# Zeros for empty rows in another buffer, and a later due time for transposes of gathered rows

## The chip, the cores and the metric

The kernel runs on one core of a Trainium2 chip. The metric is the device time of one execution in microseconds (us); the time before is the median of three runs. Matrix products run on TensorE (PE in the profile; PEld is its weight load), elementwise work on VectorE (DVE), ScalarE (ACT) and GpSimd (POOL). SyncE (SP) issues most of the DMAs, ScalarE's and GpSimd's queues issue some.

## What is computed

The reference has three stages, for 4 batches of 576 rows (2304 rows in all, 512 wide):

```
attn = attention(q, k, v, phi)              # 8 heads of 64, 32 memory slots
u    = x + real(fft over rows and columns)  # x: the heads side by side
un   = layernorm(u)
x2   = u + max(un @ w_ch1, 0) @ w_ch2       # 512 -> 2048 -> 512
e    = expert of each row: argmax of x2 @ w_gate, or the expert
       of the row before, by a gate of its own
out  = p[e] * (max(x2 @ w1[e], 0) @ w2[e])  # 8 experts, 512 -> 1024 -> 512
```

Each row goes through one expert, so the third stage sorts the rows by expert while the program runs.

## The kernel before, in words

**Products.** Precision is kept by splitting both factors into a high part of a shorter type and the rest. Every product is three matmuls (`products`, lines 1022 to 1026): high by high, high by low, low by high. A first-layer step of an expert is 12 matmuls of 256 columns, a second-layer step is 3 matmuls of 512 columns.

**Attention and Fourier stage.** For each batch, `front` (line 384 on) makes the keys and values of the memory, transposes the keys into kT (copied by ScalarE, line 446) and multiplies them with q (line 463, q loaded at line 373); `soft` (line 473 on) takes the scores through a softmax, beginning with a VectorE maximum (line 511); `back` and `mix` do the rest and write u to device memory. Meanwhile `chunks` (line 632 on) loads the weights of the second stage, which come in 64 bits: `fetch` (lines 201 to 209) takes one of the two buffers of the pool `stg` and issues a load of 512 KB on SP (line 205); ScalarE and VectorE turn it into 32 bits (lines 666 to 670, VectorE's two steps into a buffer `sw`), GpSimd multiplies the sign back, and the result is split into high and low part. Two such tasks run side by side, so the first two loads are due early.

**The zeros.** `start` (line 691 on) fills 520 columns of a buffer with zeros and stores them, on ScalarE's queue, into the last 256 rows of ys and one row behind them (lines 700 and 701). ys (N + 1 rows of 520) later takes the second stage's rows; a place of an expert's block that no row fills reads row N, so that row must hold zeros. Before, the buffer with the zeros is a buffer of the pool `stg`: the second load of weights takes the same buffer and waits on SP's queue until the stores have landed. In SP's program the order at the start is: two ph loads, two kv loads, first and second weight load, q of batch 0, third weight load, fourth weight load, and then ph, kv and q of batch 1.

**XL.** The rows of a block, turned so that the width lies on the partitions, stand in XH (high part) and XL (low part), two of each, 128 x 4 x 256. XH[0] and XL[0] are first written by `prep` for the first 256 rows, when attention and mixing are nearly done (`first_rows`, line 724).

**The experts' slots.** After the second stage the rows of each expert are cut into blocks of up to 256, one block a slot. Slots 0 and 1 are woven into the end of the second stage; from slot 2 on there is one piece of program for each slot (lines 1285 on) with two arms, full (256 rows) and narrow (up to 128). The numbers decided on the chip here give 12 slots, 0 to 11; of the ten from slot 2 on, seven are full and three (5, 6 and 11) narrow. A full slot is eight first-layer steps (`firsts`), relu and split by ScalarE and VectorE (`hiddens`), and two halves of eight second-layer steps each (`half_out`), each half ended by a VectorE product (line 1144) and a GpSimd scatter into the output (line 1147). A narrow slot has four first-layer steps with rows and weights exchanged, transposes of the result, and one half.

**What a slot does for the next.** `tokens(j + 1)` runs in slot j. GpSimd issues two indirect DMAs that gather 128 rows each from ys into a buffer of `stg` (line 1253). Each half is then turned by four TensorE transposes into the one PSUM bank pt (`turned4`, lines 288 to 297), copied by ScalarE into XH (line 1261) and subtracted by VectorE into XL (line 1263), and VectorE takes the rows' factor (line 1268). The bank is free for the second half when the subtraction of the first is done. `cuts` splits raw weights, by a ScalarE copy (line 1208) and a subtraction on VectorE or GpSimd (line 1210), and then issues the raw load for the next slot on SP (line 1200). A raw piece so has most of a slot to land.

**What sets the order.** Each engine executes its instructions in the order in which the program issues them, and this order comes from a planner that runs when the program is built (`weave`, lines 230 to 265). Tasks are generators that yield an engine, a cost in us and the planned ends of what the step depends on; the planner keeps a clock for each engine and takes next the step with the smallest planned start plus the task's bias. In the slots the costs are multiplied by SLOT_PACE (TensorE 0.928) and the biases are those of SLOTS (tokens 0.18, first 0.43, out 0.91; in the narrow arm the tokens task has 0.01). The transposes of a half are given the planned end of their gather's issue plus 3.5 as an earliest start. The program waits on the chip for what it really depends on, but in the order of the plan: a transpose that comes up on TensorE before its gather has landed holds every product behind it.

Of the kernel before, what the change touches and what calls it, by code (L numbers as in the profile page):

```python
# [9 lines left out]
F32 = mybir.dt.float32  # L10
# [157 lines left out]
def f32(ap):  # L168
    return ap.bitcast(F32)
# [3 lines left out]
def attention_fourier_experts_kernel(ctx, tc, qT, phi, kv, w1, w2, wg, wgc, wm, cs, cd, c1, c2, midx, out):  # L173
# [24 lines left out]
    stg = ctx.enter_context(tc.tile_pool(name="stg", bufs=2))  # L198
# [16 lines left out]
    def ended(*names):  # L215
        return [end.get(n, 0.0) for n in names]
# [5 lines left out]
    def span(eng, length, deps):  # L222


        start = max([clock.get(eng, 0.0)] + [d + (0.9 if eng == "D" else LAG) for d in deps])
        if eng == "T" and duty.get(start // TICK - 1, 0.0) < 0.375 * TICK:
            length *= 2
        return start, start + length

    def weave(tasks, done=lambda: False):  # L230
# [7 lines left out]
        while state and not done():  # L238
            best = None
            for s in state:  # L240
                while isinstance(s[2], float) or (callable(s[2]) and s[2]()):
                    if isinstance(s[2], float):
                        s[0] = s[2]
                    s[2] = next(s[1], None)
                if s[2] is None or callable(s[2]):
                    continue
                engs, n, deps, *share = s[2]
                n = {e: pace[e] * x for e, x in (n if isinstance(n, dict) else {engs: n}).items()}
                stop, start, eng = min((*span(e, n[e], deps)[::-1], e) for e in engs)
                if best is None or start + s[0] < best[0]:  # L250
                    best = start + s[0], s, eng, start, stop, n[eng] * (share[0] if share else 1.0)
            assert best is not None or all(s[2] is None for s in state)
            if best is not None:
                _, s, eng, start, stop, n = best
                clock[eng] = stop
                if eng == "T":
                    for k in range(int(start // TICK), int(stop // TICK) + 1):
                        part = min(stop, TICK * k + TICK) - max(start, TICK * k)
                        duty[k] = duty.get(k, 0.0) + part * n / (stop - start)
                mark["eng"] = eng  # L260
                try:
                    s[2] = s[1].send(stop + (2.0 if eng == "D" else 0.0))
                except StopIteration:
                    s[2] = None
            state[:] = [x for x in state if x[2] is not None]
# [22 lines left out]
    def turned4(src, e, bank=None, name="pt"):  # L288

        if bank is None:  # L290
            yield lambda: not mark["pt"]
            mark["pt"] = True
        e = yield "T", 0.43, [e] + (ended("pt") if bank is None else []), 0.5
        pt = (bank or ptp).tile([128, 4, 128], F32, name=name)
        for k in range(4):
            T.transpose(pt[:, k], src(k), id_)  # L296
        return pt, e

    def free_pt(e):
        mark["pt"] = False  # L300
        end["pt"] = e
# [35 lines left out]
    XL = [xx.tile([128, 4, 256], FR, name="xl0")]  # L337
# [351 lines left out]
    uu, w2h, w2l = {}, [], []  # L689

    def start():
        zr = stg.tile([128, 1040], F32, name="stg")[:, 0:520]
        yield "G", 0.5, []
        G.memset(zr, 0.0)
        G.memset(qs[:, 0:1], 0.0)
        G.memset(qs[:, 256:257], 0.0)
        yield lambda: ("kv", 0, 1) in end
        yield "D", 1.5, []
        for r in (N - 256, N - 128):
            nc.scalar.dma_start(out=ys[r:r + 128], in_=zr)  # L700
        nc.scalar.dma_start(out=ys[N:N + 1], in_=zr[0:1])
        mark["zr"] = True
# [540 lines left out]
    def tokens(j):  # L1243

        if j >= NS:
            return
        k = (NG + j) % 2
        yield lambda: ("idx", min(j, 2)) in end and (j == 0 or ("x", NG + j - 1) in end)
        x = stg.tile([128, 1040], F32, name="stg").rearrange("p (t c) -> p t c", t=2)
        e = []  # L1250
        for h in range(2):
            e.append((yield "G", 1.04, ended(("idx", min(j, 2)), ("ys", NG - 2 if j < 2 else NG - 1))))
            G.indirect_dma_start(out=x[:, h], out_offset=None, in_=ys, in_offset=IO(ap=idx[:, h, j:j + 1], axis=0),  # L1253
                                 bounds_check=N, oob_is_err=False)
        before = "first", (16 * NG - 17 if j == 0 else FFN - 1 if j == 1 else FFN + 8 * j - 9)
        yield lambda: before in end
        for h in range(2):
            pt, r = yield from turned4(lambda kk: x[:, h, 128 * kk:128 * kk + 128], e[h] + 3.5)
            hs = slice(128 * h, 128 * h + 128)
            r = yield "S", 0.5, [r] + ended(before)  # L1260
            S.copy(XH[k][:, :, hs], pt)
            r = yield "V", 0.62, [r]
            V.tensor_tensor(out=XL[k][:, :, hs], in0=pt, in1=f32(XH[k][:, :, hs]), op=ALU.subtract)
            free_pt(r)
            yield lambda: j < 2 or ("yr", 2 * (NG + j) - 3) in end
            yield "V", 0.07, []
            j8 = sm_.tile([128, 8], F32, name="j8s")
            V.scalar_tensor_tensor(out=j8, in0=x[:, h, 512:520], scalar=1.0, in1=ohs[:, j], op0=ALU.mult,
                                   op1=ALU.mult, accum_out=PV[k][:, h:h + 1])
        end["x", NG + j] = r  # L1270

    def halves(j):
# [5 lines left out]
           "w2": [chunks(extra[i::LANES], (wgt[:, 3 * i:3 * i + 2], wgt[:, 3 * i + 2])) for i in range(LANES)],  # L1278
           "gate": [gates(), gate_weights()], "sum": [sums_out()], "raw": [raws0(), raws(1), raws(2)],
           "tokens": [tokens(0), tokens(1), tokens(2)], "out": [halves(0), halves(1)],  # L1280
           "cut": [cuts(*[(j, c) for j in range(2) for c in range(8)], *[(2, c) for c in range(4)])]})

    bias.update(SLOTS)
    pace.update(SLOT_PACE)
    with ExitStack() as es:
        for j in range(2, NS):
            if j >= FIRST:
                if j == FIRST:
                    n_slots = value(tab[0:1, 2 * NS:2 * NS + 1], NS, mybir.ALL_ENGINES)
                es.enter_context(tc.If(n_slots > j))  # L1290
            half = value(tab[0:1, NS + j:NS + j + 1], 1, mybir.ALL_ENGINES)
            if j + 2 < NS:
                number(j + 2)
            ns = range(FFN + 8 * j, FFN + 8 * j + 8)
            before = dict(clock), dict(end)
            for arm in range(2):
                with (cmp.Else() if arm else tc.If(half > 0)) as cmp:  # L1297
                    own = [{"first": [firsts(ns)], "hidden": [hiddens(ns)], "out": [halves(j)]},
                           {"narrow": [narrow(j)], "turn": [turn(j)], "out": [half_out(j, 0)]}][arm]
                    weave({**own, ("tokens", "rows")[arm]: [tokens(j + 1)],  # L1300
                           ("cut", "late")[arm]: [cuts(*[(j, c) for c in range(4, 8)]), cuts(*[(j + 1, c) for c in range(4)])]})
                after = before if arm == 0 else full
                full = dict(clock), dict(end)
                for mine, theirs in zip((clock, end), after):
                    mine.clear()
                    mine.update(theirs)
                for n in ns:
                    del hid[n]
# [25 lines left out]
```

## Time and profile before

| what | us |
|---|---|
| median of three runs | 875.41 (872.26 to 875.53) |
| the profiled execution's own time | 870.53 |
| its span in the profile | 868.4 |
| TensorE busy | 797.9 (92%) |
| VectorE busy | 581.6 (67%) |
| ScalarE busy | 311.9 (36%) |
| GpSimd busy | 231.3 (27%) |

The mean granted clock of TensorE is 0.973 of full speed (1 is 2.4 GHz, 0.5 is 1.2 GHz). Attention and Fourier stage end at about 150 us, the second stage at about 605 us, and the slots from slot 2 on run from about 630 us to the end.

In the rows below, a window's line has its bounds, its length, the busy time of PE, PEld, DVE, ACT and POOL with the number of instructions in brackets, the granted clock of TensorE, the mean busy share of the 16 DMA engines and what they moved in GB/s. A line of a timeline has start, duration, engine, line of the program, operation, output <- inputs, shape, count and, in square brackets, how long the engine had stood idle and what ended it. A line of waits has the waiting engine and line, what it waited for, and the total, the number and the longest.

### The profile page before, as it was taken

What the parts mean: (1) busy time and instruction counts of PE and PEld (TensorE: products, weight loads), DVE (VectorE), ACT (ScalarE), POOL (GpSimd) and SP (SyncE); (2) the same over time, 40 slices, a digit from 0 to 9 for tenths busy, and PEclk for the clock granted to TensorE, in tenths of its full rate; (3) what the DMA queues carried; (4) which work ended last, traced back from release to release, by engine and by line L of the source; (5) the groups of instructions that cost most, each with busy time, mean ns of one, the idle gap of its engine ahead of it and who ended that gap; (6) DMA issues with size and microseconds to landing.
All of it is one profiled execution on the core that took longest, in us unless ns stands there. A gap on an engine that the chain in (4) does not pass through costs nothing. (4 is left out here: it accounts for less than half of the span.)

```text
span 868.4 us, 14567 instructions
## 1 busy us (share of the span) xinstructions
PE 797.9 (92%) x5376; PEld 690.4 (80%) x5376; DVE 581.6 (67%) x1391; ACT 311.9 (36%) x587; POOL 231.3 (27%) x194
## 2 busy tenths in 40 slices
PE   2399998899999999999999999999989997999993
PEld 1166666698989898988998989889889886888882
DVE  3677787788567867777575766667665466855563
ACT  2264454566211111111111111154445346654452
POOL 2335664588300000000000000053423311333320
PEclk8599999999999999999999999999999999999997
DMA  7976535564220000000000000392776667866655
GB/s 290 334 279 200 191 88 173 158 186 122 65 93 26 25 26 25 26 26 25 26 25 26 25 25 1 112 330 100 235 238 225 213 197 276 269 213 214 210 199 193
DMA packets 36106, 123.93 MB, mean 143 GB/s; under 512 B 5236, under 2 KB 5492, under 8 KB 34218
## 3 DMA queue, kind: packets, MB, share of 16 engines
q1 hardware_dynamic: 30216, 103.74, 35.5%
q0 software_dynamic: 4528, 14.00, 5.0%
q10 hardware_dynamic: 1266, 4.98, 1.7%
q8 instruction: 52, 0.85, 0.4%
q14 instruction: 44, 0.36, 0.1%
HBM read 107.93 MB, written 15.56 MB: 142 GB/s over the span
## 5 line engine op out<-in xcount | busy, mean ns | idle before, releaser
L1026 PE MATMUL pl<-xh,w1l 128*128 128x256 f32 x864 | 242.4, 281 | 0.0
L1024 PE MATMUL pl<-xh,w1h 128*128 128x256 f32 x576 | 162.9, 283 | 2.1 <-DVE xl L327 2.1
L1063 ACT ACTIVATE hh<-pl 128x256 fp32r<-128x256 f32 x144 | 55.4, 384 | 302.5 <-PE pl L1026 251.1
L1026 PEld LDWEIGHTS pl<-xh,w1l 128*128 128x128 f32 x864 | 163.6, 189 | 0.0
L1025 PE MATMUL pl<-xl,w1h 128*128 128x256 f32 x576 | 161.0, 280 | 0.5 <-DVE xl L327 0.5
L1208 ACT CAST w2h<-w1h 128x1024 fp32r<-128x1024 f32 x100 | 103.3, 1049 | 42.0 <-issue 32.9
L1210 DVE TENSOR_TENSOR w1l<-w1h,w2h 128x1024 fp32r<-128x1024 f32 x86 | 103.6, 1222 | 19.4 <-ACT w2h L1208 16.4
L1065 DVE SCALAR_TENSOR_TENSOR hl<-pl,hh 128x256 fp32r<-128x256 f32 x144 | 60.9, 423 | 79.2 <-ACT hh L1063 77.8
L1024 PEld LDWEIGHTS pl<-xh,w1h 128*128 128x128 f32 x576 | 108.3, 188 | 5.5 <-DVE xl L327 2.3
L1025 PEld LDWEIGHTS pl<-xl,w1h 128*128 128x128 f32 x576 | 108.5, 188 | 3.7 <-DVE xl L327 0.8
L1024 PE MATMUL y<-w2h,hh 128*128 128x512 f32 x272 | 108.9, 400 | 1.9 <-ACT hh L1063 1.9
L1026 PE MATMUL y<-w2h,hl 128*128 128x512 f32 x272 | 106.9, 393 | 0.2 <-DVE hl L1065 0.2
L1025 PE MATMUL y<-w2l,hh 128*128 128x512 f32 x272 | 106.7, 392 | 0.0
L778 DVE SCALAR_TENSOR_TENSOR jk<-stg,wgt 128x512 bf16<-128x512 f32 x144 | 99.0, 687 | 2.7
L317 POOL TENSOR_TENSOR rv<-rv,C 128x1 f32<-128x1 f32 x18 | 13.1, 730 | 274.1 <-DVE rv L315 268.9
L1024 PE MATMUL pl<-xh,w2h 128*128 128x256 f32 x288 | 83.4, 290 | 0.5 <-DVE w2l L1065 0.5
L1025 PE MATMUL pl<-xl,w2h 128*128 128x256 f32 x288 | 81.6, 283 | 0.0
L1147 POOL DMA_INDIRECT out_dram<-u,idx x21 | 27.3, 1302 | 154.6 <-DVE u L1144 105.6
L1024 PE MATMUL y<-w2h,w2l 128*128 128x512 f32 x168 | 67.2, 400 | 0.0
L1026 PE MATMUL y<-w2h,w2l 128*128 128x512 f32 x168 | 66.2, 394 | 0.0
L1025 PE MATMUL y<-w1l,w2l 128*128 128x512 f32 x168 | 66.1, 393 | 0.0
L1026 PEld LDWEIGHTS y<-w2h,hl 128*128 128x128 f32 x272 | 51.1, 188 | 12.6 <-DVE hl L1065 1.3
(240 smaller groups left out, 1435.4 us busy)
## 6 DMA issues: line engine op xcount, KB each, us to landing
w1h<-in_wm_dram SPq DMA_DIRECT2D x108, 512.0 KB
stg<-in_w_dram SPq DMA_DIRECT2D x21, 512.0 KB
kvt<-in_kv_dram SPq DMA_DIRECT2D x8, 1290.0 KB
wgt<-in_w_dram SPq DMA_DIRECT2D x11, 512.0 KB
ys<-stg SPq DMA_DIRECT2D x9, 520.0 KB
qt<-in_qT_dram SPq DMA_DIRECT2D x4, 1156.0 KB
ph<-in_phi_dram SPq DMA_DIRECT2D x8, 320.0 KB
u<-ut SPq DMA_DIRECT2D x12, 192.0 KB
```

The lines of the kernel that those rows point to most:

```text
L317: G.tensor_tensor(out=rv, in0=rv, in1=c_("half"), op=ALU.pow)
L778: V.scalar_tensor_tensor(out=jk, in0=yt[:, t, 0:512], scalar=1.0, in1=wgt[:, e], op0=ALU.mult, op1=ALU.mult, accum_out=L[:, t, e:e + 1])
L1024: T.matmul(ps, a[0], b[0], start=first, stop=False)
L1025: T.matmul(ps, a[0], b[1], start=False, stop=False)
L1026: T.matmul(ps, a[1], b[0], start=False, stop=last)
L1063: S.activation(out=hh, in_=ps, func=AF.Relu)
L1065: V.scalar_tensor_tensor(out=hl, in0=ps, scalar=0.0, in1=f32(hh), op0=ALU.max, op1=ALU.subtract)
L1147: G.indirect_dma_start(out=out, out_offset=IO(ap=idx[:, h, j:j + 1], axis=0), in_=o, in_offset=None, bounds_check=N - 1, oob_is_err=False)
L1208: S.copy(WH[c], RAW[c])
L1210: E[mark["eng"]].tensor_tensor(out=WL[c], in0=RAW[c], in1=f32(WH[c]), op=ALU.subtract)
```

## The change

The zeros are written into XL[0], seen as 128 x 1024 of 32 bits, and stored to ys from there; the pool `stg` loses this use, so its two buffers go to the first two weight loads. In `tokens`, the earliest start of the transposes becomes the planned end of the gather's issue plus 6.0 where j is above 2, which is what slots 2 and later run; for j up to 2 it stays 3.5. Line numbers behind the first edit grow by one.

```
@@ -689,7 +689,8 @@
     def start():
-        zr = stg.tile([128, 1040], F32, name="stg")[:, 0:520]
+
+        zr = f32(XL[0]).rearrange("p k c -> p (k c)")[:, 0:520]
         yield "G", 0.5, []
         G.memset(zr, 0.0)
...
@@ -1255,7 +1256,7 @@
         for h in range(2):
-            pt, r = yield from turned4(lambda kk: x[:, h, 128 * kk:128 * kk + 128], e[h] + 3.5)
+            pt, r = yield from turned4(lambda kk: x[:, h, 128 * kk:128 * kk + 128], e[h] + (6.0 if j > 2 else 3.5))
             hs = slice(128 * h, 128 * h + 128)
```

## Rows read from the trace of the kernel before

**Rows 1.** Windows of 10 us: bounds, length, busy (count) by engine, clock, DMA share, GB/s
```profile
30.00:40.00 10.00, 1.53 (x5) 0.83 (x5) 9.55 (x20) 3.70 (x6) 4.38 (x6) 0.50 0.91 349
...
60.00:70.00 10.00, 10.00 (x50) 7.62 (x49) 8.40 (x22) 3.66 (x8) 6.06 (x7) 1.00 0.46 184
```

**Rows 2.** Waits of TensorE from 630 us on: total us, times, longest us
```profile
PE pt L296 <- DMA stg<-ys,idx: 12.0, 12, 2.9
...
PE pl L1026 <- issue: 3.5, 1, 3.5
```

**Rows 3.** Timeline of SP's queue, 2 to 30 us: start, duration, operation
```profile
2.62 13.07 SPq L205 DMA_DIRECT2D stg<-in_w_dram  x2
...
15.74 0.43 SPq L373 DMA_DIRECT2D qt<-in_qT_dram  x1
```

**Rows 4.** Waits of SP's queue, whole execution
```profile
SPq L205 <- DMA ys<-stg: 12.2, 2, 11.5
```

**Rows 5.** Windows of 2 us at the start, columns as rows 1
```profile
8.00:10.00 2.00, 0.54 (x12) 0.51 (x16) 1.37 (x2) 1.33 (x2) 0.00 (x0) 1.00 1.01 428
...
12.00:14.00 2.00, 1.57 (x40) 1.30 (x40) 0.33 (x2) 0.09 (x1) 0.00 (x0) 1.00 0.77 298
...
14.00:16.00 2.00, 0.74 (x4) 0.40 (x4) 1.86 (x4) 1.25 (x2) 1.13 (x2) 1.00 0.02 9
```

**Rows 6.** Timeline of all engines, 0 to 45 us
```profile
13.91 0.66 ACT L666 ACTIVATE stg<-stg 128x512 f32<-128x512 f32 x1 [3.76 <-DMA stg<-in_w_dram]
...
19.31 0.43 DVE L669 TENSOR_SCALAR sw<-stg 128x512 uint32<-128x512 uint32 x1 [3.17 <-DMA stg<-in_w_dram]
...
20.65 0.35 ACT L446 COPY kT<-pfr 128x256 f32<-128x256 f32 x1
...
22.23 1.22 PE L463 MATMUL pfr<-qt,kT 64*32 64x289 f32 x16 [6.89 <-DMA qt<-in_qT_dram]
...
26.56 0.69 DVE L511 TENSOR_REDUCE mx<-sc 97x16 f32<-97x512 f32 x1 [3.83 <-PE sc L505]
```

**Rows 7.** Timeline of TensorE, three windows: transposes in slots 2, 3, 4
```profile
640.07 0.63 PE L296 MATMUL pt<-C,stg 128*128 128x128 f32 x4 [2.85 <-DMA stg<-ys,idx]
...
665.27 0.63 PE L296 MATMUL pt<-C,stg 128*128 128x128 f32 x4 [0.17 <-DMA stg<-ys,idx]
...
690.65 0.63 PE L296 MATMUL pt<-C,stg 128*128 128x128 f32 x4 [1.77 <-DMA stg<-ys,idx]
```

**Rows 8.** Timeline of VectorE from 600 us on
```profile
630.19 0.75 DVE L1144 TENSOR_SCALAR u<-y,pv 128x512 f32<-128x512 f32 x1 [1.42 <-PE y L1026]
...
658.06 0.75 DVE L1144 TENSOR_SCALAR u<-y,pv 128x512 f32<-128x512 f32 x1 [4.81 <-PE y L1026]
...
681.79 0.75 DVE L1144 TENSOR_SCALAR u<-y,pv 128x512 f32<-128x512 f32 x1 [4.80 <-PE y L1026]
...
707.12 0.75 DVE L1144 TENSOR_SCALAR u<-y,pv 128x512 f32<-128x512 f32 x1 [4.82 <-PE y L1026]
...
695.57 0.68 DVE L1263 TENSOR_TENSOR xl<-pt,xh 128x512 fp32r<-128x512 f32 x1
...
720.33 0.68 DVE L1263 TENSOR_TENSOR xl<-pt,xh 128x512 fp32r<-128x512 f32 x1
...
722.71 0.75 DVE L1144 TENSOR_SCALAR u<-y,pv 128x512 f32<-128x512 f32 x1 [0.42 <-PE y L1026]
```

**Rows 9.** Window of 2 us behind the longest wait, columns as rows 1
```profile
642.00:644.00 2.00, 2.00 (x12) 2.00 (x11) 0.55 (x4) 0.85 (x2) 0.00 (x0) 0.50 0.80 270
```

**Rows 10.** Window of slot 8 ahead of its first transposes, columns as rows 1
```profile
765.40:772.60 7.20, 7.20 (x61) 7.10 (x60) 5.11 (x8) 4.27 (x7) 4.67 (x3) 1.00 0.54 152
```

**Rows 11.** The gathers (line 1253), whole execution, issue to landing
```profile
DMA to landing us min/median/max: 3.6/5.6/7.9
```

**Rows 12.** Waits of TensorE in slot 5, then in slot 11
```profile
PE pt L296 <- DMA stg<-ys,idx: 2.0, 2, 1.0
...
PE pt L296 <- DMA stg<-ys,idx: 1.6, 2, 1.0
```

More of the change, by code (lines that the diff above doesn't have):

```diff
@@ L691, in start @@
     def start():
-        zr = stg.tile([128, 1040], F32, name="stg")[:, 0:520]
+        zr = f32(XL[0]).rearrange("p k c -> p (k c)")[:, 0:520]
         yield "G", 0.5, []
@@ L1257, in tokens @@
         for h in range(2):
-            pt, r = yield from turned4(lambda kk: x[:, h, 128 * kk:128 * kk + 128], e[h] + 3.5)
+            pt, r = yield from turned4(lambda kk: x[:, h, 128 * kk:128 * kk + 128], e[h] + (6.0 if j > 2 else 3.5))
             hs = slice(128 * h, 128 * h + 128)
```

## The prediction

> **What bounds the kernel now.** I read the windows of the early stage first, because the zeros are used there. At 30 to 40 us TensorE is busy 1.53 of 10 us and VectorE 9.55; at 60 to 70 us TensorE is busy all 10 [rows 1]. So up to some 43 us a chain through several engines sets the time, and after that TensorE does, up to its last product. Whatever shortens the chain moves everything behind it forward; later, a gain must be idle time of TensorE, or time at its lower clock.
>
> Next the waits of TensorE in the stage of the experts' slots. One line is large: the transposes of gathered rows (line 296) wait for the gather's DMA 12 times, 12.0 us in all. Beside it stands one stop of 3.5 us that no wait explains; nothing else is of that size [rows 2]. These slots are bound by TensorE and interrupted by the gathers.
>
> Then SP's queue at the start. Two weight loads stand there as one piece of 13.07 us, and the first q load is issued only at 15.74 [rows 3]. The queue's waits say why: the second load waited 11.5 us until the stores of zeros into ys had landed [rows 4], since the zeros filled one of the two stg buffers. The 2 us windows show the price: the DMA engines move 428 GB/s at 8 to 10 us and are at a share of 0.02 at 14 to 16 us [rows 5]. In the timeline TensorE waits 6.89 us, until 22.23, for that q; VectorE's first step on the scores follows at 26.56 [rows 6].
>
> **The zeros.** Nothing is added: the same memset and the same three stores, with XL[0] as source. XL[0] is next written by the preparation of the first rows, at the end of attention, more than 100 us later; that wait costs nothing. Removed is the 11.5 us wait of line 205 [rows 4]. SP then issues the second weight load at about 3.0 us and q at 3.4, right behind the first. The third load still waits for the first load's buffer, but q now stands ahead of it.
>
> When does q land? In the old order the first weights had landed at 13.91 [rows 6], about as the queue ran dry: a share of 0.77 over 12 to 14 us ends it near 13.5 [rows 5], so I count 0.4 us for landing. The second weights (0.52 MB) and q (1.18 MB) now follow without a gap: 1.71 MB at 428 GB/s are 4.0 us, so q lands at 13.5 + 4.0 + 0.4 = 17.9. At the 298 GB/s of 12 to 14 us [rows 5], when zeros were moving too, it would be 5.7 us and 19.6. kT must be ready as well: it is copied at 20.65, on ScalarE's queue behind the second weights, for whose landing (about 19.3) VectorE and ScalarE waited [rows 6]. These weights now land near 15.1, and two ScalarE steps of some 0.7 us bring kT to about 17. So TensorE starts this step at 17.9 instead of 22.23, 4.3 us earlier, or 2.6 at the slow rate. I take 4.0, near the fast end, because the engines kept that rate whenever only loads were queued; the lower bound is none, if something off this chain holds the front.
>
> Does it last? The next ph, kv and q loads stand behind the fourth weight load on SP and are issued earlier by about the same amount; VectorE then runs almost without a gap (9.55 of 10) into the stretch in which TensorE is full [rows 1]. I see nothing fixed in time that could swallow the gain. **Sum: -4.0 us, ends 0 and -4.3.**
>
> The Trainium skill ("DMA: Bandwidth & Descriptors", section "Specifications") gives about 358 GB/s as the HBM limit of a NeuronCore; by it the 1.71 MB would take 4.8 us and the gain would be 3.5. The windows show 428 here [rows 5], so I stay with the row.
>
> **The transposes.** Only tokens(j) with j above 2 changes, so slots 2 to 11: ten of them, seven with both halves and three narrow (5, 6 and 11). No DMA moves on its own: the gathers stay where they are on POOL. What moves is, per half, four transposes, one ScalarE copy, one VectorE subtraction and the short PV step; VectorE and ScalarE cuts may swap places with them, and with these cuts SP's raw loads, which have most of a slot to land.
>
> First what a wait is worth. In slots 2, 3 and 4 the first transposes waited 2.85, 0.17 and 1.77 us for the gather [rows 7], and nothing else in these slots did. VectorE's last step of a slot gives the slots' lengths: 630.19 to 658.06 to 681.79 to 707.12, so 27.87, 23.73 and 25.33 us [rows 8]. Slots 3 and 4 less their waits are both 23.56: a wait counts one to one, and nothing else was waiting to take its place. Slot 2 less 2.85 is 25.02, 1.46 too long: behind this wait the granted clock is 0.50, the 1.2 GHz level, in the window of 642 to 644 us [rows 9].
>
> Then how far they move. Due times go up by 2.5 us of the planner's time, in which a first-layer product costs 1.41 x 0.928 = 1.31. Ahead of the first transposes TensorE does five such products, 60 matmuls in 7.2 us of slot 8 [rows 10], some 1.42 us each. The new due time lets two more pass: 2.84 us of real work. That is just the longest wait. A median gather takes 5.6 us to land and the worst 7.9 [rows 11], and the second halves move by as much as the first.
>
> So in the full slots the whole wait goes: 12.0 less the 2.0 and 1.6 of narrow slots 5 and 11 [rows 12] is 8.4, and 1.5 of clock with slot 2's wait: -9.9. If only one product passed (1.42 us), 2.85 would keep 1.43, and 1.77 and its like 0.3 to 0.4: about -7. Above is no more to win.
>
> What is late next: the rows of the next slot. In full slots there is room: slot 4's second subtraction ends at 696.25, more than 10 us ahead of 707.12 [rows 8]. In narrow slots there is not: in slot 5 it ends at 721.01, and VectorE takes the slot's last product at 722.71 [rows 8]; 1.7 us of slack for a shift of 2.8. There the next slot's first product may wait about 1.1 us, at the ends of slots 5 and 6; slot 11 has none behind it. VectorE is nearly full there too, so it may hold slot 11's last step. Of the 3.6 us of waits in narrow slots I keep 1.5; the ends are a gain of 3.6 (nothing is late) and a loss of 1.5 (2.0 won in slot 5, 1.1 lost at each of two boundaries and some 1.3 to the clock behind them, nothing won in slot 11). **Sum: -9.9 - 1.5 = -11.4 us.**
>
> **Total: -15.4 us.** The profiled execution took 870.53 us (span 868.4 and 2.1 around it), 4.9 below the median of the runs shown, 875.41. I carry the difference over: 875.4 - 15.4 = **860.0**.
>
> **Rivals.**
> 1. The front gains little: the loads behind the kv transfers crowd them, or ScalarE holds kT. Against it, the empty stretch at 14 to 16 us; for it, that a rate of 298 GB/s did occur. With 1 us left of 4: 863.0. Chance 0.17.
> 2. The transposes find the next wait: one product instead of two passes, or the pt bank's round over ScalarE and VectorE stands among the second-layer products. Half of 11.4 stays: 875.4 - 4.0 - 5.7 = 865.7. For it, ScalarE's cuts and copies share one queue; against it, slot 3 with almost no wait. Chance 0.11.
> 3. The second edit doesn't do what it says: the gathers are served later too and the waits remain. Then only the front is left: 871.4, not to be told from no change (about 0.5% is what a measurement of this kernel can tell). The landing times speak against it, as they don't depend on TensorE. Chance 0.09, which takes in smaller mishaps of the first edit as well.
> 4. Slower: the second half's rows come after the slot's last product, in full slots also, and TensorE idles at every boundary. Price: 2.85 and 1.46 as in slot 2, at nine boundaries, 38.8 us against the 15.4: 898.8. It decides once the second subtraction slides by more than 10 us in full slots. Only the narrow slots are near that point. Chance 0.05.
>
> **Numbers.** The forecast itself has 0.58. Faster is 0.58 + 0.17 + 0.11 = 0.86, same 0.09, slower 0.05. The range runs from the best ends (4.3 + 9.9 + 3.6 = 17.8, so 857.6, and 2.6 lower because the runs shown scatter that far below their median: the lowest was 872.26) to 869, above rivals 1 and 2 with the weaker ends of both: 855 to 869. Left out are rivals 3 and 4.
>
> **What would show it.** SP's wait for ys gone, q issued before 4 us, TensorE's wait at that step 2 to 3 us instead of 6.89, and the first step on the scores near 22.5. Waits of line 296 for the gather under 1 us in all; full slots all near 23.6 us, slot 2 without a stretch of half clock. Waits of the first product for xl behind slots 5 and 6, about 1 us. I am wrong if q lands after 20, if a full slot stays above 24.2, or if a new wait of the products stands in the slots.

## The result and the profile after

The changed kernel took **860.41 us** (median; 859.00 to 862.83). The kernel before, beside it on the same chip, took 873.84 (863.64 to 875.53). The ratio is 0.9879, with a 95% interval of 0.9837 to 0.9922. Run again later, beside another set of runs of the kernel before, it took 861.51, ratio 0.9858 (0.9827 to 0.9889). By the two intervals the change is worth 7 to 15 us.

The profiled execution after has a span of 857.2 us against 868.4, so 11.2 us went. I follow them in the order of the prediction. Line numbers behind the first edit are one higher.

SP's queue at the start; columns as in [rows 3]:

```profile
2.61 1.81 SPq L205 DMA_DIRECT2D stg<-in_w_dram  x2
4.86 0.33 SPq L373 DMA_DIRECT2D qt<-in_qT_dram  x1
```

The two weight loads, one piece of 13.07 us in [rows 3], are now issued in 1.81, and q at 4.86 instead of 15.74. The wait for ys of [rows 4] is gone, and no engine waits for the stores out of XL anywhere. These stores themselves are issued on ScalarE's queue at 9.40 us, as before.

Windows of 2 us, columns as in [rows 5]:

```profile
10.00:12.00 2.00, 1.83 (x36) 1.26 (x28) 0.00 (x0) 0.13 (x1) 0.00 (x0) 1.00 0.95 335
12.00:14.00 2.00, 1.49 (x32) 1.52 (x36) 0.00 (x0) 0.06 (x1) 0.00 (x0) 1.00 1.01 347
14.00:16.00 2.00, 0.97 (x20) 0.54 (x12) 1.41 (x5) 1.52 (x3) 0.29 (x1) 1.00 1.03 422
```

The empty stretch at 14 to 16 us (9 GB/s in [rows 5]) is filled. But from 10 to 14 us, with the DMA engines at a share of 0.95 to 1.01, only 335 and 347 GB/s move, not the 428 that the sum used.

The timeline of the front, rows that answer to [rows 6], and one more:

```profile
17.03 0.36 ACT L446 COPY kT<-pfr 128x256 f32<-128x256 f32 x1
...
19.30 1.22 PE L463 MATMUL pfr<-qt,kT 64*32 64x289 f32 x16 [3.12 <-DMA qt<-in_qT_dram]
...
23.62 0.69 DVE L511 TENSOR_REDUCE mx<-sc 97x16 f32<-97x512 f32 x1 [3.39 <-PE sc L505]
...
41.27 1.96 PE L573 MATMUL pbk<-cdt,vT 64*32 64x512 f32 x16 [1.19 <-DMA cdt<-in_cd_dram]
```

kT is ready at 17.03 as forecast, but q at 19.30, not 17.9. The scores come 2.94 us earlier (23.62 against 26.56). Then the last row shows something new: TensorE waits 1.19 for the table cdt. Before, this product started at 42.96 without a wait; so of 2.94 us 1.69 are left there, and VectorE's first product of the experts' stage comes at 610.48 instead of 612.60, 2.12 earlier.

TensorE's waits in the slots, 612 to 870 us, as [rows 2]:

```profile
PE pl L1027 <- issue: 3.5, 1, 3.5
PE y L1026 <- DVE w1l L1211: 2.2, 3, 0.7
PE y L1098 <- ACT u L1091: 0.9, 3, 0.3
PE pl L1025 <- issue: 0.4, 2, 0.2
PE pt L296 <- DMA stg<-ys,idx: 0.2, 1, 0.2
```

The waits for gathers are down from 12.0 to 0.2 us. Counted in the timeline, the first transposes of a full slot now stand behind 84 first-layer matmuls in place of 60, so two more products of 12 pass ahead of them, as forecast; the second halves stand behind 96 in place of 84, one product more. The stop of 3.5 that no wait explains is still there. In place of the gathers stand 2.2 us for a weight cut, three times 0.7: once in each narrow slot.

VectorE's last products of slots 1 to 4 answer to [rows 8]:

```profile
628.07 0.75 DVE L1145 TENSOR_SCALAR u<-y,pv 128x512 f32<-128x512 f32 x1 [1.42 <-PE y L1027]
...
651.75 0.75 DVE L1145 TENSOR_SCALAR u<-y,pv 128x512 f32<-128x512 f32 x1 [4.81 <-PE y L1027]
...
675.16 0.75 DVE L1145 TENSOR_SCALAR u<-y,pv 128x512 f32<-128x512 f32 x1 [4.82 <-PE y L1027]
...
698.53 0.75 DVE L1145 TENSOR_SCALAR u<-y,pv 128x512 f32<-128x512 f32 x1 [4.82 <-PE y L1027]
```

Slots 2, 3 and 4 take 23.68, 23.41 and 23.37 us (27.87, 23.73 and 25.33 before). All slots in one table:

| slots 2 to 11 | before | after | difference | forecast |
|---|---|---|---|---|
| seven full, sum | 174.69 | 163.79 | -10.9 | -9.9 |
| narrow 5, 6, 11 | 15.59, 19.16, 15.06 | 15.74, 19.81, 15.73 | +1.5 | -1.5 |
| start of the slots | 612.60 | 610.48 | -2.1 | -4.0 |

With 0.35 us more behind the last slot this is the 11.2 of the spans.

What happens in a narrow slot is seen in slot 5, in the timeline of GpSimd, VectorE and TensorE:

```profile
708.97 2.39 POOL L1211 TENSOR_TENSOR w1l<-w1h,w2h 128x1024 fp32r<-128x1024 f32 x1 [5.06 <-ACT w2h L1209]
...
710.14 1.23 DVE L1269 SCALAR_TENSOR_TENSOR j8s<-stg,ohs 128x8 f32<-128x8 f32 x1
...
711.31 1.21 DVE L1211 TENSOR_TENSOR w1l<-w1h,w2h 128x1024 fp32r<-128x1024 f32 x1
...
712.58 0.50 PE L1026 MATMUL y<-w1l,w2l 128*128 128x512 f32 x1 [0.72 <-DVE w1l L1211]
...
714.27 0.73 DVE L1145 TENSOR_SCALAR u<-y,pv 128x512 f32<-128x512 f32 x1
```

With the later due time the planner gave GpSimd one cut in each narrow slot (17 cuts in all against 14). While it runs, VectorE's small step j8s (the rows' factor, 0.16 us where no cut of GpSimd runs) takes 1.23 and ends with GpSimd's cut, at 711.37 against 711.36. VectorE's own cut comes after it, and TensorE waits 0.72 for that one. The last row also has no wait in its brackets: VectorE comes late to the slot's last product, not TensorE.

The stretched step is not peculiar to narrow slots. In each full slot of the changed kernel GpSimd makes a cut too, and one j8s beside it takes 1.29 or 1.30, here in slot 2 (ends at 644.54 and 644.51):

```profile
641.60 2.91 POOL L1211 TENSOR_TENSOR w1l<-w1h,w2h 128x1024 fp32r<-128x1024 f32 x1 [5.03 <-ACT w2h L1209]
...
643.24 1.30 DVE L1269 SCALAR_TENSOR_TENSOR j8s<-stg,ohs 128x8 f32<-128x8 f32 x1
```

There no wait of TensorE for a cut follows; a full slot has room on VectorE.

The Trainium skill ("SBUF — State Buffer", section "SBUF: two separate sides") says that VectorE and GpSimd share a pair of ports as an exclusive lock, and that a VectorE step with two inputs in SBUF is blocked for as long as the GpSimd instruction that holds it runs. By that the step should end with the GpSimd cut, and the trace agrees (711.37 and 711.36).

### The profile page after: what moved, and what is told of

Its sections match the earlier page's. It is cut to its first block, busy times and chain, and to the rows that moved or that the text cites. A ratio compares the mean times of both kernels' runs of the same rounds, so it can differ in the third digit from the quotient of the medians.

```text
span 857.2 us, 14558 instructions
## 1 busy us (share of the span) xinstructions
PE 796.2 (93%) x5376; PEld 687.5 (80%) x5376; DVE 588.9 (69%) x1391; ACT 311.8 (36%) x584; POOL 240.6 (28%) x197
## 3 DMA queue, kind: packets, MB, share of 16 engines
q10 hardware_dynamic: 1266, 4.98, 1.9%
## 5 line engine op out<-in xcount | busy, mean ns | idle before, releaser
L1211 DVE TENSOR_TENSOR w1l<-w1h,w2h 128x1024 fp32r<-128x1024 f32 x83 | 100.9, 1220 | 18.7 <-ACT w2h L1209 15.3
L1027 PE MATMUL y<-w2h,hl 128*128 128x512 f32 x272 | 106.9, 393 | 0.2 <-DVE hl L1066 0.2
L1211 POOL TENSOR_TENSOR w1l<-w1h,w2h 128x1024 fp32r<-128x1024 f32 x17 | 44.9, 2645 | 83.9 <-ACT w2h L1209 83.9
```

Source lines behind the costliest of these rows:

```text
L1027: T.matmul(ps, a[1], b[0], start=False, stop=last)
L1211: E[mark["eng"]].tensor_tensor(out=WL[c], in0=RAW[c], in1=f32(WH[c]), op=ALU.subtract)
```

## Experiments

Eleven runs, each timed beside the kernel before (runs of one session share these); there is one profile of each. Slots are measured as above, between VectorE's last products. "q" is TensorE's start on q, "cdt" its first product with that table, "slots" VectorE's first product of the experts' stage.

| run | time, ratio (95%) | q | scores | cdt | slots | full, sum | narrow, sum |
|---|---|---|---|---|---|---|---|
| before | | 22.23 | 26.56 | 42.96 | 612.60 | 174.69 | 49.81 |
| after | 860.41, 0.988 (0.984 to 0.992) | 19.30 | 23.62 | 41.27 | 610.48 | 163.79 | 51.28 |
| e1_zeros | 870.13, 0.998 (0.995 to 1.001) | 20.24 | 24.56 | 41.66 | 612.73 | 171.03 | 48.43 |
| e2_due | 862.23, 0.989 (0.985 to 0.992) | 22.88 | 27.20 | 43.60 | 615.76 | 163.27 | 52.84 |
| e3_full_only | 860.82, 0.986 (0.982 to 0.990) | 19.78 | 24.10 | 43.96 | 615.06 | 163.41 | 51.97 |
| e4_cdt_early | 860.73, 0.987 (0.983 to 0.990) | 19.70 | 24.02 | 40.41 | 610.55 | 164.12 | 51.49 |
| e5_narrow_v | 860.04, 0.988 (0.981 to 0.995) | 18.75 | 23.07 | 39.47 | 609.45 | 163.63 | 51.59 |
| e6_zeros_late | 879.70, 1.008 (1.005 to 1.011) | 22.34 | 27.41 | 44.58 | 631.14 | 169.07 | 52.16 |
| e7_due475 | 866.19, 0.995 (0.992 to 0.998) | 18.41 | 22.74 | 40.41 | 610.21 | 166.59 | 54.04 |
| e8_due85 | 864.27, 0.993 (0.990 to 0.995) | 19.84 | 24.17 | 41.33 | 610.87 | 166.07 | 53.72 |
| e9_stores_later | 859.17, 0.984 (0.981 to 0.987) | 16.91 | 21.78 | 38.17 | 608.02 | 163.65 | 53.53 |
| e10_both_front | 860.59, 0.986 (0.982 to 0.989) | 18.46 | 23.60 | 40.00 | 611.24 | 163.43 | 53.07 |
| e11_after_again | 861.51, 0.986 (0.983 to 0.989) | 18.80 | 23.13 | 39.53 | 612.22 | 163.47 | 52.53 |

Two columns need care. The stop that no wait explains sits at the change from slot 5 to slot 6 (3.2 to 4.1 us in all executions) and at some of the other changes between full and narrow slots (0.2 to 1.6); the narrow sums swing with it by 1 to 2 us. And executions of one kernel differ in the start of the slots: after and e11_after_again are the same program, at 610.48 and 612.22. So a difference of 2 us between two single profiles shows little by itself.

**The first edit alone.**

```
-        zr = stg.tile([128, 1040], F32, name="stg")[:, 0:520]
+        zr = f32(XL[0]).rearrange("p k c -> p (k c)")[:, 0:520]
```

> The first edit alone: zeros in XL[0], the transposes due at +3.5 as before. My theory: the two edits act in different stages and simply add. q lands near 19.3 us as in the changed kernel, the scores start near 23.6 instead of 26.56, the load of the cosine table then makes TensorE wait about 1.2 us, and some 2.1 us are left at the slots; the gathers' waits in the slots stay as before (some 8 to 14 us in all). Time 0.25% under the kernel before. Rival: everything after the front hangs on something that did not move, and the time is the same to 0.1%.

The front does what it does in the changed kernel: scores 2.0 us earlier, a wait of 0.6 for cdt. But its slots begin at 612.73, no earlier than those of before (612.60), against the 2.1 us that the theory left there. In the whole time 1.5 us are left (0.17% of 872.26), and the interval (0.995 to 1.001) includes no gain at all. The waits for gathers stay:

```profile
PE pt L296 <- DMA stg<-ys,idx: 9.7, 11, 1.9
```

In this execution slot 2 waited only 0.5 and had no half clock behind it; so a single wait belongs to the execution, but their sum (12.0 before, 9.7 here) to the kernel.

**The second edit alone.**

```
-            ... turned4(..., e[h] + 3.5)
+            ... turned4(..., e[h] + (6.0 if j > 2 else 3.5))
```

> The second edit alone: later due time, zeros in the weights' buffer as before. My theory: the seven full slots from slot 2 on take 23.4 us each as in the changed kernel, the three narrow ones 15.7 to 19.8, the waits for the gathers are under 0.5 us in all; the front is as before, with TensorE waiting 6.9 us for q. Span about 2.1 us above that of the changed kernel (857.2), so near 859.3. Rival: the zeros' buffer also changes the gathers (they use the same pool), and the slots come out longer than in the changed kernel by a microsecond or more.

The front still waits for q (4.98 us), no wait for a gather is left in the slots, full slots take 23.07 to 23.48, and the time is 10.0 us lower. The same wait for a cut as in the changed kernel stands in its place:

```profile
PE y L1025 <- DVE w1l L1210: 2.2, 3, 0.7
```

So some 10 us of the 11 to 12 come from the second edit: nearly all of the gain is the due time. That the first adds its 1.5 fits, but neither its own run nor the difference between this run and the changed kernel is clear of the noise.

**The dose: 4.75 and 8.5 in place of 6.0.**

```
-            ... e[h] + (6.0 if j > 2 else 3.5))
+            ... e[h] + (4.75 if j > 2 else 3.5))
```

> Both edits with 4.75 in place of 6.0, so that one first-layer product fewer passes ahead of the transposes in full slots. Theory (each product that passes hides 1.42 us of the gather's landing): waits for the gather come back where they were above 1.4 (slots 2, 4 and the like), 0.3 to 1.5 each, 2 to 4 us in all; the full slots with them are as much longer, the others 23.4. The time is 2 to 4 us above the changed kernel. Rival (the plan's new order, not the passing products, shortens the slots): all full slots stay at 23.4 or all return to 23.7 and above, whatever the waits.

```
-            ... e[h] + (6.0 if j > 2 else 3.5))
+            ... e[h] + (8.5 if j > 2 else 3.5))
```

> Both edits with 8.5 in place of 6.0, two more products ahead of the transposes. Theory: full slots stay at 23.4 (nothing is left to hide, and the rows still come in time); in the narrow slots the rows for the next slot come late, and the first product behind slots 5 and 6 waits 1 to 3 us for xl, so the time is 1 to 6 us above the changed kernel. Rival (late rows were never near, since the planner puts the turn of the rows first on VectorE in narrow slots): no wait for xl, and the time is the same within 1.5 us.

TensorE's waits in the slots, first with 4.75, then with 8.5:

```profile
PE y L1026 <- POOL w1l L1211: 3.6, 3, 1.4
PE pt L296 <- DMA stg<-ys,idx: 2.7, 4, 1.2
```

```profile
PE pt L296 <- DVE xl L1264: 4.8, 7, 1.4
```

With 4.75 the first transposes stand behind 72 matmuls, six products, and the waits for gathers come back in slots 2, 4, 5 and 8, 2.7 us in all and 2.3 of it in full slots. So the sum over full slots goes 8.4, 2.3, 0.2, 0 for due times of 3.5, 4.75, 6.0 and 8.5: products that pass hide the landing one by one, as the theory had it. The time is 5.8 us above the changed kernel, more than expected; 2.8 of it is in the full slots, and 2.8 in the narrow ones, where TensorE now waits for GpSimd's cut itself.

With 8.5 both theories missed, although the time fell into the first one's range. No product waits for late rows at the start of a slot; instead the transposes of the second half wait for the bank pt, which the first half's subtraction frees: 0.2 in four of the full slots, 1.4 in each narrow one. Full slots also grow by 0.3 each, more than their waits. The time is 3.9 above the changed kernel. The value 6.0 stands between two limits, the landing on one side and the bank's round on the other.

**Only full slots get the later due time.**

```
-    def tokens(j):
+    def tokens(j, arm=0):
...
-            ... e[h] + (6.0 if j > 2 else 3.5))
+            ... e[h] + (6.0 if j > 2 and arm == 0 else 3.5))
...
-                    weave({**own, ("tokens", "rows")[arm]: [tokens(j + 1)],
+                    weave({**own, ("tokens", "rows")[arm]: [tokens(j + 1, arm)],
```

> Both edits, but the later due time only in the full arm; the narrow arm keeps +3.5. In the changed kernel the narrow slots got no shorter although their waits for gathers went: 15.74, 19.81 and 15.73 us against 15.59, 19.16 and 15.06. My theory: the new order of the narrow arm costs as much as the waits did (a cut that went to GpSimd, and a VectorE step that stands beside it), so with the old order they return to about 15.6, 19.2 and 15.1 with waits for gathers of 1 to 4 us, and the span is 1 to 1.5 us under 857.2. Rival: the narrow slots are long because the shorter full slots leave the cuts and raw loads less time; then they stay at 15.7 and above with any order, and the span does not fall.

TensorE's waits for gathers in the slots of this run:

```profile
PE pt L296 <- DMA stg<-ys,idx: 3.3, 4, 1.0
```

Narrow slots lose the wait for a cut and get their gather waits back (1.9 in slot 5, 1.4 in slot 11). Less all waits and stops, slots 5 and 11 take 13.5 to 13.8 us in the old order (before, e1_zeros and this run) and 14.3 to 14.6 in the new one, so what the new order saves in waits it pays back. The time is that of the changed kernel, not 1 to 1.5 less as the theory had it: in narrow slots the edit is worth nothing that shows, and my 1.5 us of gain there were wrong. The rival is not excluded: slots 5 and 6 took 16.65 and 20.45 here, no less than in the changed kernel, with 4.9 of stops.

**GpSimd out of the narrow slots' cuts.**

```
-            yield from cut(j, c)
+            yield from cut(j, c, use)
...
-  [cuts(*[(j, c) for c in range(4, 8)]), cuts(*[(j + 1, c) for c in range(4)])]
+  [cuts(*[(j, c) for c in range(4, 8)], use=("GV", "V")[arm]), cuts(*[(j + 1, c) for c in range(4)], use=("GV", "V")[arm])]
```

> Both edits; in the narrow arm the weight cuts all go to VectorE. Theory (the later due time made the planner give GpSimd one cut per narrow slot, and while it runs VectorE's small row-factor step takes 1.2 us instead of 0.16 and holds the next cut, for which TensorE waits 0.7): the factor steps are all near 0.16, the 0.7 us wait of the second-layer products for a cut is gone in the narrow slots, and these are 0.5 to 1 us shorter each: 15.0, 19.1, 15.0 against 15.7, 19.8, 15.7 in the changed kernel. Rival (VectorE is simply full in a narrow slot): the cut that comes back costs it 1.2, so the wait of TensorE for cuts stays at 0.5 to 1.2 and the slots keep their length. The time moves by under 2 us either way.

```profile
709.15 0.16 DVE L1269 SCALAR_TENSOR_TENSOR j8s<-stg,ohs 128x8 f32<-128x8 f32 x1
...
711.64 0.50 PE L1026 MATMUL y<-w1l,w2l 128*128 128x512 f32 x1 [0.78 <-DVE w1l L1211]
```

The small step is back at 0.16, so the cut on GpSimd did stretch it. But the cut that VectorE takes over costs as much, and TensorE still waits 0.78. The rival's signs came: the wait stays and the slots keep their length, as they would if VectorE had no room left in a narrow slot. Which engine does that cut does not matter.

**Zeros stored later, and the plan with them.**

```
-        yield lambda: ("kv", 0, 1) in end
+        mark["zr"] = True
+        yield lambda: ("sT", 0) in end
...
-        mark["zr"] = True
```

> Both edits; the three stores of the zeros are issued only behind the scores' copies of batch 0. Theory (q landed 1.4 us later than forecast because the zeros moved beside the second weights and q): q lands near 18, the first step on the scores stands near 22.3 instead of 23.6, and the windows from 10 to 16 us show above 400 GB/s. Rival (the loads' own queue sets it): q lands within 0.5 us of 19.3 as before. In both the whole time changes by no more than 2 us from the changed kernel, since the wait for the cd table takes what the front gains.

This run missed what it was for: 19.3 us slower than the changed kernel by the medians (its profile, the slowest of its ten executions, by 27.5). With the stores out of the planner's way the weight tasks start earlier in its plan, and a third piece's two ScalarE steps were put ahead of the copy of kT:

```profile
21.93 0.35 ACT L446 COPY kT<-pfr 128x256 f32<-128x256 f32 x1
...
22.34 1.46 PE L463 MATMUL pfr<-qt,kT 64*32 64x289 f32 x16 [1.39 <-ACT kT L446]
```

kT comes 4.9 us later than in the changed kernel, and behind it the whole attention is in another order: 17.3 us more between the first product with cdt (44.58) and the experts' stage (631.14). Its windows from 10 to 14 us do show 390 and 392 GB/s.

Slot 2 of this profile, with the due time at 6.0, shows a limit of the second edit:

```profile
661.88 0.63 PE L296 MATMUL pt<-C,stg 128*128 128x128 f32 x4 [3.31 <-DMA stg<-ys,idx]
```

The gather was issued 6.6 us behind slot 1's last product (5.4 in the changed kernel's profile) and took 6.5 to 6.8 to land, and the slot took 28.33. Two products hide the landing in most profiles, not in all; in e4_cdt_early slot 2 waited 0.5 as well.

A few words that change what the planner sees can cost more than this change gains, so the next two runs move only the DMA instructions and leave every planned step.

**The stores alone issued later, plan unchanged.**

```
     def start():
...
-        for r in (N - 256, N - 128):
-            nc.scalar.dma_start(out=ys[r:r + 128], in_=zr)
-        nc.scalar.dma_start(out=ys[N:N + 1], in_=zr[0:1])
         mark["zr"] = True
...
         end["sT", b] = r
+        if b == 0:
+            zr = f32(XL[0]).rearrange("p k c -> p (k c)")[:, 0:520]
+            for r0 in (N - 256, N - 128):
+                nc.scalar.dma_start(out=ys[r0:r0 + 128], in_=zr)
+            nc.scalar.dma_start(out=ys[N:N + 1], in_=zr[0:1])
```

> Both edits, and the three stores of the zeros alone are issued later, behind the scores' copies of batch 0 on the same queue; every other instruction keeps its place. Theory (the zeros moving beside the second weights and q cost the front 1 to 1.5 us of the forecast): the 2 us windows from 10 to 14 us show 380 GB/s or more in place of 335 and 347, TensorE starts on q near 18, the first step on the scores stands at 22.3 to 22.8 instead of 23.6, and the wait for the cd table grows by what q gained, so the slots begin no earlier than 610.0. Rival (q's own queue or kT sets it): q at 19.3 within 0.4. Time within 1.5 us of the changed kernel in both.

The windows of 2 us, and below them TensorE and VectorE in the front:

```profile
10.00:12.00 2.00, 2.00 (x44) 1.84 (x40) 0.00 (x0) 0.02 (x1) 0.00 (x0) 1.00 0.97 388
12.00:14.00 2.00, 1.68 (x36) 1.31 (x28) 0.20 (x2) 1.36 (x2) 0.00 (x0) 1.00 1.07 412
14.00:16.00 2.00, 0.74 (x4) 0.40 (x4) 1.86 (x5) 1.88 (x4) 1.00 (x2) 1.00 0.91 384
```

```profile
16.91 1.22 PE L463 MATMUL pfr<-qt,kT 64*32 64x289 f32 x16 [1.44 <-DMA qt<-in_qT_dram]
...
21.78 0.69 DVE L516 TENSOR_REDUCE mx<-sc 97x16 f32<-97x512 f32 x1 [2.25 <-PE sc L510]
...
38.17 1.96 PE L578 MATMUL pbk<-cdt,vT 64*32 64x512 f32 x16
```

With no zeros beside them the loads run at 388 and 412 GB/s in place of 335 and 347. This does not hang on one profile: over 10 to 14 us the eight with the stores in the new buffer at their old time have a mean of 336 to 364, the three with later stores 386 to 400. q is there at 16.91, and the slots begin 4.6 us earlier than in the one profile of before. The scores come 4.87 behind q (4.32 in the changed kernel), since ScalarE's step on the weights now stands ahead of their copy and itself waits for GpSimd:

```profile
18.18 0.62 ACT L689 CAST w1h<-sw 128x512 fp32r<-128x512 f32 x1 [2.23 <-POOL sw L686]
18.70 0.69 ACT L468 COPY sT<-pfr 128x289 f32<-128x289 f32 x2
```

The cd wait did not grow, against the expectation; with the zeros out of the way there is none here. In this profile the narrow slots gave 2.3 of it back, with two more stops of 1.1 that no wait explains.

**The cd table loaded early, alone and with the stores later.** In the first run its load moves to ScalarE's queue right behind the scores' copies; in the second the zeros follow behind it.

```
-        nc.scalar.dma_start(out=cdt, in_=cd)
...
         end["sT", b] = r
+        if b == 0: nc.scalar.dma_start(out=cdt, in_=cd)
```

> Both edits, and the load of the cosine table for the columns is issued on ScalarE's queue right behind the copies of the first scores, some 9 us earlier; no other engine's order changes. My theory: of the 2.9 us that the front gains at the scores, 1.2 are given back at TensorE's first product with this table, which now waits for its load; with the load earlier this wait goes, this product starts near 40.1 instead of 41.27, and the span is about 1.2 us under 857.2. Rival: the next thing late (the exponentials of the second batch, or its kv load, pushed back by the table) takes the wait over, and the span stays.

> As the run with the later stores, and the load of the cd table is issued ahead of them, right behind the scores' copies. Theory (the front's gain of 4 was lost to the zeros' traffic and to the wait for the cd table, in equal parts): the cd wait is gone, the scores stand near 22.5 and the first product with the cd table at 38.9 to 39.5, and the slots begin 1.5 to 2.5 us earlier than in the changed kernel, near 608.5; the time is 1.5 to 2.5 lower. Rival (behind the front another limit takes the gain, as the run with the earlier cd load suggested when its first product came 0.9 earlier and its slots at the same 610.5): the slots begin at 610 to 611 all the same and the time is that of the changed kernel within 1 us.

The wait for cdt is gone in both: the product comes 16.4 us behind the scores, as in the kernel before (42.96 less 26.56); in the changed kernel's first profile it was 17.65. But the slots begin at 610.55 and 611.24, no earlier than the changed kernel's 610.48, and neither time moved. In the second run the rival came out, nearly (its slots were to begin by 611): q was there only at 18.46 and the scores 5.14 behind it, so the product with cdt came no earlier than 40.00. From there to the slots it took 571.24, against 569.21 in the changed kernel's first profile; 1.0 of this lies ahead of 143 us, and 1.3 at a wait for a gather ahead of the slots (below).

**The changed kernel once more.**

> The changed kernel itself once more, for a second profile on the chip of these runs. Expected within 2 us of its first 860.4; full slots 23.2 to 23.7, narrow slots 15.7, 19.8 and 15.7 within 0.5, and the wait of 0.7 for a cut in each of them, if these belong to the kernel and not to one execution; q at 19.3 within 0.5 if its landing does.

Full slots (23.20 to 23.41) and the wait of 0.72 for a cut in each narrow slot repeat; q is at 18.80. The narrow slots took 15.90, 21.22 and 15.41, the middle one 1.4 more than was expected, of which the stop has 0.2. There is no wait for cdt this time (16.4 us from the scores). It stands in five of the seven profiles with the first edit, stores and this load in their old place (0.6 to 3.4 us), and in neither of the two without the edit; so it comes with the earlier front, but not in every execution. The first product with cdt comes at 39.53, 1.7 us ahead of the first profile, and yet the slots begin 1.7 later. Two places account for most of it. The first is the end of the attention, in windows of 10 us; first this run, then the changed kernel's first profile:

```profile
140.00:150.00 10.00, 7.93 (x42) 7.07 (x41) 6.82 (x18) 1.72 (x4) 3.60 (x5) 0.83 0.56 167
150.00:160.00 10.00, 7.25 (x45) 5.89 (x44) 6.33 (x12) 5.86 (x11) 4.59 (x5) 0.91 0.59 210
160.00:170.00 10.00, 10.00 (x56) 9.16 (x55) 6.53 (x12) 4.86 (x9) 4.29 (x4) 0.75 0.35 96
```

```profile
140.00:150.00 10.00, 7.93 (x49) 6.44 (x47) 7.83 (x21) 2.76 (x6) 3.03 (x5) 1.00 0.58 167
150.00:160.00 10.00, 6.46 (x39) 4.93 (x38) 5.42 (x11) 5.29 (x11) 4.52 (x5) 1.00 0.58 211
160.00:170.00 10.00, 8.93 (x63) 8.16 (x64) 8.55 (x13) 5.38 (x10) 5.64 (x5) 1.00 0.33 97
```

In one execution TensorE's granted clock is partly at half speed here (0.83, 0.91, 0.75), in the other at full. From the last transposes of the attention's rows (un into pfr, at 141.30 and 142.62) to the first of the kind (un into pt) behind 196 us the first takes 59.65 and the other 57.76, so 1.9 went here.

The second place is the gathers ahead of the slots, whose due time the change leaves at 3.5; the changed kernel's first profile, this run, and e10_both_front:

```profile
569.42 0.63 PE L296 MATMUL pt<-C,stg 128*128 128x128 f32 x4 [0.22 <-DMA stg<-ys,idx]
...
571.20 0.63 PE L296 MATMUL pt<-C,stg 128*128 128x128 f32 x4 [1.42 <-DMA stg<-ys,idx]
...
570.22 0.63 PE L296 MATMUL pt<-C,stg 128*128 128x128 f32 x4 [1.48 <-DMA stg<-ys,idx]
```

From the last transposes of un (503 to 509 us) to the slots it takes 106.8 to 106.9 in the three profiles with 1.4 to 1.5 of this wait (e2_due, e10_both_front, e11_after_again), and 105.1 to 106.0 in the other nine that keep this order.

From the first product with cdt to the slots these twelve need 569.2 to 572.7. The four with full clock between 140 and 170 us (before, after, e5_narrow_v and e7_due475) need 569.2 to 570.0, the other eight, with a mean of 0.83 to 0.94 there, 569.5 to 572.7. The clock alone does not order them: e10_both_front, at 0.83 over 140 to 150 us, passes that stretch in 57.53, and e8_due85 and e9_stores_later, at 0.94, need 569.5 and 569.9 in all. So what the front wins can arrive at the slots, and up to 3.5 us of it can be lost on the way, to the clock, to a gather, and to differences in the attention ahead of 143 us that were not followed up.

## Why the prediction was right, and where not

**The time and the sign.** 860.41 lies 0.4 from the forecast, and the range held it. That is better than the sum deserves: it foresaw 15.4 us less, the profiles show 11.2 and the ratios 10.6 and 12.4. The absolute number came out because the forecast started from 875.41, and the kernel before had medians of 870.97 to 874.12 in the later runs. In the range one step does not come out: the lowest time, 872.26, lies 3.15 below the median of 875.41, not 2.6; that would move the lower bound from 855 to 854.5 and changes nothing else.

**Full slots: right.** Forecast -9.9, found -10.9; the second edit alone gave 10.0 in time. Both parts are shown: two products pass in the first halves (one, not two, in the second), the waits go by dose, and slot 2 has no half clock once its wait is gone. The extra 1.0 is some 0.15 us in each full slot beside its wait: less their waits, slots 3, 4, 8 and 9 of before took 23.53 to 23.59, those of after 23.37 to 23.41.

**Front: the mechanism right, the size wrong.** The step that failed is "the engines kept that rate whenever only loads were queued". The zeros' stores were queued too, since only their place of waiting had changed; the sum had this case as its slow rate (298 GB/s, q at 19.6) and chose the other end. It also counts 1.71 MB, without the zeros' own 0.53 MB; at 428 GB/s these are 1.2 us, about the 1.4 by which q came late, so the runs do not separate a lower rate from more bytes. Measured: 335 and 347 GB/s, q at 19.30. Over the eight profiles with the first edit and the stores in their old place q starts at 18.41 to 20.24, in the two with the stores later and the plan kept at 16.91 and 18.46 (means 19.4 and 17.7). The other failing sentence is "I see nothing fixed in time that could swallow the gain": the load of cdt took 1.2 of it in the first profile and up to 3.4 in another, the stretch with a lower granted clock 1.9 in e11_after_again, and a gather ahead of the slots 1.4 to 1.5 in three runs. In the time, the front's gain is not clear of the noise (e1_zeros). The Trainium skill's limit of about 358 GB/s ("DMA: Bandwidth & Descriptors", section "Specifications") is not what held the loads: the windows after show 422 GB/s at 14 to 16 us, and 388 to 412 once the zeros were out of the way.

**Narrow slots: wrong in sign and in mechanism.** Forecast -1.5 and a wait of about 1.1 for the next slot's rows behind slots 5 and 6; found +1.5 and no such wait, not even at 8.5. The sign is not one execution's: less the stops, the narrow slots take 46.3 and 44.9 in the old order (before, e1_zeros), 47.1 in e3_full_only, and 47.4 to 48.5 in the eight profiles with 6.0 in both arms. The step that failed is the room of VectorE. The text said "VectorE is nearly full there too", but held it against slot 11's last step only. The gather waits of 3.6 go (2.0 in slot 5, 1.6 in slot 11; slot 6 had none); against them stand 2.2 for the cuts, 0.3 more for a ScalarE step, 0.4 of small stops, and 2.3 that no wait names (1.0 in slot 5, 1.1 in slot 11, 0.25 in slot 6). The runs with the old order there and without GpSimd's cut show that the slots keep their length either way. What the 2.3 are was not settled; VectorE's late last product, and short gaps around transposes, are only seen in the timeline.

**Rivals.** The second half of rival 2, the bank's round among the second-layer products, is real but begins only behind 6.0: 4.8 us at 8.5. Of rival 1 the front's shortfall came at about two thirds of its size in the first profile (1.9 of 3 us). Rival 3 did not come: the gathers' waits went from 12.0 to 0.2. Rival 4 had late rows as its trigger, which no run showed.

**The marks.** q issued before 4 us: 4.86, missed. TensorE's wait for q 2 to 3 us: 3.12, just above. Scores near 22.5: 23.62, missed. q not after 20: 19.30, though 20.24 in e1_zeros. Waits for gathers under 1 us: 0.2. Full slots near 23.6: 23.18 to 23.68. The sign of being wrong, a new wait of the products in the slots, did appear, with 0.72 in each narrow slot.

## What to carry to other kernels

A wait that counts one to one is best attacked by its dose: count what passes in front of it, and try one step on either side, since here a due time 1.25 lower brought back 5.8 us and one 2.5 higher brought 3.9 through another resource. Look also for the places that the edit leaves out: the gathers ahead of the slots kept the old due time, and three runs lost 1.4 to 1.5 us there. When a transfer is moved out of the way of others, ask whether it still shares the engines with them: freeing the buffer let q be issued 11 us earlier, but the zeros went on beside it and q came 1.7 us later on average than with their stores issued later (eight profiles against two). Where a planner writes the order, an edit that changes what it sees is two edits; move the instruction alone when its effect is to be read.

The kernel with the stores later had the lowest median (859.17, ratio 0.984) and the earliest slots, but its interval overlaps that of the changed kernel beside it (0.981 to 0.987 against 0.983 to 0.989): only its lead over the kernel before is shown.

## What the runs showed of the hardware

- A VectorE step of 0.16 us took 1.23 beside a GpSimd subtraction, and ended with it (711.37 and 711.36), and so in the full slots (1.30, 644.54 and 644.51); the subtraction right before the former, with one input in PSUM, ran under the same GpSimd cut in 0.69, as elsewhere.
- TensorE's granted clock fell to 0.50 behind the wait of 2.85 us [rows 7, 9], and in other executions of the same order it is at 0.83 or 1.00 over 140 to 150 us with the same 7.93 us of TensorE's time busy. Over 20 to 60 us its mean is 0.65 to 0.72 in seven of the thirteen profiles and 1.00 in the other six.
- At the change from slot 5 to 6 TensorE stops for 3.2 to 4.1 us in every profile, and in no run did an edit move it. It is longer than the 2.1 us that the front won at the slots; its cause was not tried.
